# First attention of an attention-then-feed-forward kernel: roots on ScalarE, chunk additions on GpSimd, integer additions of the weights on VectorE

## The chip, the core and the metric

The kernel runs on one core of a Trainium2 chip. A core has five engines, each with its own queue of instructions, worked off strictly in order: TensorE (PE; its weight loads are shown as PEld), VectorE (DVE), ScalarE (ACT), GpSimd (POOL) and SyncE (SP, which here only issues DMAs). Engines wait for each other through semaphores. The metric is the device time of one execution in microseconds, the median of three runs.

## The reference

Attention over 8 batches and 12 heads, 448 tokens, 64 channels, with RMS norms of q and k; then a feed-forward block with a squared ReLU over the 3584 tokens.

```python
def rmsnorm(x, g):
    rms = np.sqrt(np.mean(x * x, axis=-1, keepdims=True) + 1e-06)
    return x / rms * g
q_n, k_n = (rmsnorm(q, g_q), rmsnorm(k, g_k))
scores = 1.0 / np.sqrt(64) * np.matmul(q_n, k_n.transpose(0, 1, 3, 2))
attn = np.exp(scores - np.max(scores, axis=-1, keepdims=True))
attn = attn / (np.sum(attn, axis=-1, keepdims=True) + 1e-09)
x = np.matmul(attn, v)           # (8, 12, 448, 64) -> (3584, 768)
...
h = x @ w_in                     # 768 -> 2048
g = np.maximum(h, 0.0) ** 2
out = g @ w_out                  # 2048 -> 768
```

The weights w_in and w_out come in double precision, everything else in single.

## The kernel before

**Stages.** The work goes in four spans of two batches each. A span has an attention over 12 pairs of heads, then the first product (with w_in, below "L1") and the second product (with w_out), both by a Strassen-like scheme of seven products of blocks in place of eight. Attention of the later spans is woven into the second product of the span before. The attention of the first span has nothing to be woven into: `attention_alone` runs it by itself, with `NAT` = 12 pairs, and L1 of span 0 follows. Beside these two stages the weights are prepared.

**One iteration of `attention_alone`** (pair i) is written out by hand as an order of instructions; each engine's queue has its share of it, in that order. There are four parts, with a `yield` behind each, and at each yield the caller puts in one or two quarter steps of the weight preparation:

1. scores of key chunks 0 and 1 (L771 on PE, into two PSUM tiles) and their exponentials (L775 on ACT, with k's root as the scale); the transposes of k of pair i+1 (L746 on PE, copied by L748 on ACT); the second half of the values of pair i-1 (L829); `add_up(i, 1)`, the sum of chunks 0 and 1 on DVE (L788); `norm(i + 2)`.
2. the transposes of q of pair i+1, moved to SBUF by ACT (L750); the load of the next v.
3. scores and exponentials of chunks 2 and 3; `total_of(i - 1)` on PE (L854): the sums of the exponentials over the keys, by matmuls with ones; the first half of the values; `finish(i - 1)` on DVE: a transpose of the totals (L867), their reciprocal (L868), a transpose back (L869) and the multiplication of the attention's result (L878).
4. in some iterations a second `add_up` on DVE; `combine_x(i - 1)`, sums for the products, on DVE (L888 to L893).

**The norm** (L702 to L711) squares q and k on ACT, sums on DVE (L703), scales and adds epsilon on DVE (L704), takes the power -0.5 on POOL (L706, 112 x 16 numbers) and multiplies q by it on POOL (L708). For pairs 0, 1 and 2 `normalise_in_turn` (L332 to L340) does the same for q and k one after the other, with q's multiplication on DVE.

**Totals.** `total_of` adds up by matmuls, two per tensor (each shows as two records): the DVE sum of chunks 0 and 1, and each chunk left. With odd i (but the last) the second `add_up` has put chunk 2 into the DVE sum too, so two tensors are left, 8 records; with even i and the last there are three, 12 records.

**Order of q.** q and k are loaded with four tokens in each of 112 partitions, so token 4p+j stands at column j*112+p behind the transposes; `finish` writes the result with a stride of four to bring the tokens back into order.

**The weights.** Each of 32 blocks of doubles is rounded to single precision by integer operations: ACT makes the high word's magnitude (L578) and scales the low word (L594), DVE clamps, shifts and joins (L591, L596, L601), and POOL adds both as integers, in two halves of 384 columns (`value`, L566). For every second block POOL makes four sums of blocks (`total`, L572), and SP writes seven block matrices to DRAM (w1s or w2s), from where the products load them as `sw`. A block takes four quarter steps: 13 blocks' worth (`EARLY` = 52 quarter steps) beside the first attention, the rest beside L1, at 88 quarter steps in 50 products.

**L1** (L1044 on PE). For each of eight f there are seven products of 6 matmul records, in the order pa, pb, pc, pd, pa, pd, pc by the names of the PSUM tiles. pb, pc and pd take two PSUM banks in turn, so pd takes the bank of pb, and may start when DVE has taken pb's result (L1051, into z). Other results are taken by L1054 and L1059 on DVE, and by ACT, which then does ReLU (L1016) and square (L1018).

Of the kernel before, what the change touches and what calls it, by code (L numbers as in the profile page):

```python
# [2 lines left out]

# [304 lines left out]
    return qk[:, first:second + 1:second - first]  # L308


def load_q(nc, qk, q, i):

    _, H, S, D = q.shape
    b, h0 = divmod(2 * i, H)
    nc.sync.dma_start(places_of(qk, i, 0)[:S // 4, 0].rearrange("p (h e) -> p h e", h=2),
                      q[b, h0:h0 + 2].rearrange("h (p j) d -> p h (j d)", j=4))
# [8 lines left out]
        nc.sync.dma_start(dst[:, :, h], k[b, h0 + h].rearrange("(p j) d -> p j d", j=4))  # L325


def normalise_in_turn(nc, raw, sq, rstd, mhalf, between=lambda: None):

    SP, _, n = rstd.shape  # L330
    for s in range(2):
        nc.scalar.activation(sq[:, s], raw[:, s], AF.Square)  # L332
        nc.vector.tensor_reduce(rstd[:, s], sq[:, s].rearrange("p (n d) -> p n d", n=n), AX, ALU.add)
        nc.vector.tensor_scalar(rstd[:, s], rstd[:, s], float(n) / sq.shape[2], 1e-6, ALU.mult, ALU.add)
        nc.gpsimd.tensor_tensor(rstd[:, s], rstd[:, s], mhalf[:SP, 0:n], ALU.pow)
        if s == 0:
            between()
            nc.vector.tensor_tensor(sq[:, 0].rearrange("p (j h d) -> p h j d", j=n // 2, h=2),
                                    raw[:, 0].rearrange("p (h j d) -> p h j d", j=n // 2, h=2),
                                    rstd[:, 0].rearrange("p (h j) -> p h j ()", h=2)  # L340
                                    .to_broadcast([SP, 2, n // 2, sq.shape[2] // n]), ALU.mult)


def first_pair(tc, q, k, g_q, g_k, held):
# [24 lines left out]
    with tc.tile_pool(name="ps_first", bufs=1, space=bass.MemoryType.PSUM) as ps_first:  # L369

        nc.vector.memset(qkT[:, 1], 0.0)
        idle = ps_first.tile([2 * D, S], F32, name="idle")
        for _ in range(3):
            nc.tensor.matmul(idle, qkT[:, 1, 0, 0:2 * D], qkT[:, 1, 1], start=True, stop=True)
        normalise_in_turn(nc, raw, sq, rstd, mhalf, between)
        for s, src in ((1, raw[:, 1]), (0, sq[:, 0])):
            pt = ps_first.tile([2 * D, S], F32, name=f"pt{s}")
            for j in range(NJ):
                nc.tensor.transpose(pt[:, j * SP:(j + 1) * SP], src[:, j * 2 * D:(j + 1) * 2 * D], ident[:SP, :SP])
            if s:  # L380
                nc.scalar.copy(qkT[:, 0, s], pt)
            else:
                nc.scalar.activation(qkT[:, 0, s], pt, AF.Copy, scale=gains[:, 0:1])


@with_exitstack
def attention_then_ffn_bounded(
# [128 lines left out]
    def blocks_of(n):  # L516
        at = n // 2 % BLOCKS * 8 * HW
        return stage[:, at:at + 8 * HW].rearrange("p (k m) -> p k m", k=8)

    def exponents_of(n):  # L520
        at = BLOCKS * 8 * HW + n % EXPS * NW
        return stage[:, at:at + NW]
# [23 lines left out]
    def prepare(t):  # L546
# [10 lines left out]
        def value(n, half):  # L557
            if not there(n):
                return

            to = ((A11, A12), (A21, A22)) if n < NFC else ((A11, A21), (A12, A22))
            dst = blocks_of(n)[:, to[n % 2][half]]
            part = slice(half * HW, (half + 1) * HW)
            if doubles:
                _, eu, low, _ = parts(n)
                nc.gpsimd.tensor_tensor(*[x.bitcast(I32) for x in (dst, low[:, part], eu[:, part])], ALU.add)  # L566
            else:
                nc.gpsimd.tensor_copy(dst, words_of(n).bitcast(F32)[:, part])

        def total(n, dst, x, y, op):  # L570
            if there(n) and n % 2:
                nc.gpsimd.tensor_tensor(*[blocks_of(n)[:, i] for i in (dst, x, y)], op)  # L572

        def unsigned(n):

# [7 lines left out]
        if there(n) and n % 2:  # L583
            c = n % NFC // 2
            dst = w1s[c] if n < NFC else w2s[:, c // 4, :, c % 4]
            nc.sync.dma_start(dst.rearrange("k p m -> p k m"), blocks_of(n)[:, 0:7])
            written[0] = n + 1
        if there(t) and doubles:
            e, eu, low, high = parts(t)
# [103 lines left out]
    def norm(i):  # L693
# [8 lines left out]
        nc.scalar.activation(sq, raw, AF.Square)  # L702
        nc.vector.tensor_reduce(rstd, sq.rearrange("p s (n d) -> p s n d", d=D), AX, ALU.add)  # L703
        nc.vector.tensor_scalar(rstd, rstd, 1.0 / D, 1e-6, ALU.mult, ALU.add)  # L704
        flat = rstd.rearrange("p s n -> p (s n)")
        nc.gpsimd.tensor_tensor(flat, flat, mhalf[:SP, 0:4 * NJ], ALU.pow)  # L706

        nc.gpsimd.tensor_tensor(sq[:, 0].rearrange("p (j h d) -> p h j d", j=NJ, h=2),  # L708
                                raw[:, 0].rearrange("p (h j d) -> p h j d", j=NJ, h=2),
                                rstd[:, 0].rearrange("p (h j) -> p h j ()", h=2).to_broadcast([SP, 2, NJ, D]),  # L710
# [31 lines left out]
    def transpose(i, s, n):  # L742

        pt = bank("pt", n)
        for j in range(NJ):
            nc.tensor.transpose(pt[:, j * SP:(j + 1) * SP], normed[i][s][:, j * P:(j + 1) * P], ident[:SP, :SP])  # L746
        if s:
            nc.scalar.copy(qkT[:, i % 2, s], pt)  # L748
        else:
            nc.scalar.activation(qkT[:, i % 2, s], pt, AF.Copy, scale=gains[:, 0:1])  # L750

    def scores(i, c):

# [26 lines left out]
    def add_up(i, c):  # L780

        acc = acc_of(i)
        if i >= NAT and c == NF:
# [2 lines left out]
                nc.vector.tensor_tensor(part, part, probs[i, c][rows], ALU.add)  # L786
            return
        nc.vector.tensor_tensor(acc, probs[i, 0] if c == 1 else acc, probs[i, c], ALU.add)  # L788

    def fold(i):  # L790

# [48 lines left out]
                    nc.tensor.matmul(into, vs[i][rows, h, c, :], probs[i, c][rows, h, :],  # L840
                                     start=(c == 0), stop=(c == NF), skip_group_check=True)

    def added(i):

        return 3 if i % 2 and i + 1 < NAT else 2

    def total_of(i):


        tots[i] = ps_o.tile([P, S], F32, tag="t", name="tot")  # L850
        parts = [acc_of(i)] + [probs[i, c] for c in range(added(i), NJ)]
        for n, pr in enumerate(parts):
            for h in range(2):
                nc.tensor.matmul(tots[i][h * D:(h + 1) * D, :], sums["ones"], pr[:, h, :],  # L854
                                 start=(n == 0), stop=(n + 1 == len(parts)))

    def finish(i):
# [4 lines left out]
        if i < NAT:  # L862
# [5 lines left out]
            nc.vector.reciprocal(few, turned.rearrange("p (g r) -> p g r", r=32)[:, :, 0])  # L868
            nc.vector.transpose(factors.rearrange("p (g r) -> p g r", r=32),  # L869
                                few.rearrange("p g -> p g ()").to_broadcast([P, S // 32, 32]))  # L870

            x = x.rearrange("d (p j) -> d j p", j=NJ)
            pav, factors = (t.rearrange("d (j p) -> d j p", j=NJ) for t in (pav, factors))
        else:
            rest = rests.pop(i)
            nc.vector.tensor_tensor(rest, pav, rest, ALU.add)
# [18 lines left out]
    def attention_alone():  # L895


        for i in range(NAT):
# [5 lines left out]
            if i == 0:  # L904
# [6 lines left out]
                norm(2)  # L911
                load_v(1)
                values(0, (0, 1))
                load(3)
                yield
                continue
# [10 lines left out]
            if more:  # L927
                transpose(i + 1, 0, 0)
            load_v(i + 1)
            yield  # L930
            scores(i, 2)
            scores(i, 3)
# [1 line left out]
            values(i, (0, 1))  # L934
            finish(i - 1)
            yield
            if added(i) == 3:
                add_up(i, 2)
            combine_x(i - 1)
            if NAT <= i + 3 < NAT + 2:  # L940
                load(i + 3)
# [210 lines left out]
    with tc.tile_pool(name="words", bufs=2) as spare["pool"]:  # L1152
# [5 lines left out]
        with tc.tile_pool(name="first", bufs=2, reuse_waits="tile") as work:  # L1158
# [1 line left out]
            free = [gT[:, f] for f in range(NFC) if f % HF < HF - 2]  # L1160
            places[:] = [g.rearrange("p (h q) -> p h q", h=2) for g in free[:2 * NJ]]
            sums[0], sums[1] = (g.rearrange("p (h q) -> p h q", h=2) for g in free[2 * NJ:2 * NJ + 2])
            sums["turned"], sums["factors"] = (g[:, 0:S] for g in free[2 * NJ + 2:2 * NJ + 4])
            sums["ones"] = work.tile([SP, D], F32, tag="ones", name="ones", bufs=1)
            nc.vector.memset(sums["ones"], 1.0)
            for u, _ in enumerate(attention_alone()):

                weights(min(EARLY, 4 + (EARLY - 4) * u // (4 * NAT - 7)))
# [39 lines left out]
def kernel(  # L1208
# [40 lines left out]
    )  # L1249
    with tc.manual_schedule():  # L1250

        nc.vector.memset(top, 0.0)
        nc.scalar.activation(top, top, AF.Exp)
        first_pair(tc, q, k, g_q, g_k, held)

    bits = nc.values_load(top.bitcast(mybir.dt.int32))
# [37 lines left out]
```

## Time and profile before

| what | value |
|---|---|
| median of three runs | 1365.82 us (1364.13 to 1366.27) |
| the profiled execution | 1362.09 us, its span on the core 1360.0 us |
| granted TensorE clock | 0.998 |
| instructions | 16939 |
| root on POOL, L706 | 9 x 3242 ns = 29.2 us |
| q's multiplication on POOL, L708 | 9 x 1413 ns = 12.7 us |
| integer additions on POOL, L566 | 34 x 1139 ns, 20 x 1226 ns, 10 x 1248 ns |
| block sums on POOL, L572 | 64 x 1167 ns = 73.5 us |
| chunk additions on DVE in the first attention, L788 | 17 x 1465 ns = 24.8 us |

A row names the line, the engine, the operation, what it writes and reads, and gives its count and the mean time of one. A duration holds everything from the start of the instruction on its engine to its end, so also the time in which a started instruction stands still for another engine. Starts are in microseconds from the beginning of the span. Neighbouring instructions of an engine overlap by some 0.1 us in the records. The page's busy shares are unions of such durations, over the whole span; windows give them for a stretch.

### The profile page before, as it was taken

The page shows a single profiled execution, that of the slowest core. Times are in us where ns is not written, and L with a number is a line of the kernel's source. Part 1 is how long each engine was busy: PE and PEld are TensorE (multiplying, and loading weights), DVE is VectorE, ACT ScalarE, POOL GpSimd, SP SyncE. Part 2 cuts the span into 40 slices and gives each one's busy share as a digit, 9 for nine tenths or more (in the row PEclk, how much of TensorE's full clock was granted, in tenths as well). Part 3 has the DMA queues.
Part 4 walks back from the last instruction along what each step waited for, and adds up shares of the span by engine and source line. Part 5 has one row for each costly group of instructions (what it writes and reads, how often), then busy time and mean ns, then how long its engine had stood idle before and what let it go on. Part 6 is the DMA issues. An engine that isn't in the chain of part 4 may idle for free.

```text
span 1360.0 us, 16939 instructions
## 1 busy us (share of the span) xinstructions
PE 1340.6 (99%) x5618; PEld 642.3 (47%) x5618; DVE 815.2 (60%) x1436; ACT 426.8 (31%) x657; POOL 636.8 (47%) x505
## 2 busy tenths in 40 slices
PE   8989999999999999999999999999999999999998
PEld 3333455444444455444444455444444455555554
DVE  6989776499987333567778523557788633332111
ACT  7876466433332011233332111233333211110000
POOL 6998887466573122655564222546566312220000
PEclk9999999999999999999999999999999999999999
DMA  9687999665675433355675433345665443234443
GB/s 250 192 235 196 300 379 330 180 132 110 130 149 127 102 89 88 96 119 118 137 150 114 113 100 87 101 104 117 144 128 111 103 103 87 87 91 107 104 114 70
DMA packets 434085, 190.12 MB, mean 140 GB/s; under 512 B 282949, under 2 KB 430789, under 8 KB 433989
## 3 DMA queue, kind: packets, MB, share of 16 engines
q1 hardware_dynamic: 427364, 180.33, 52.3%
q0 software_dynamic: 4736, 8.40, 2.4%
q8 instruction: 47, 0.77, 0.2%
q10 hardware_dynamic: 1888, 0.23, 0.1%
q14 instruction: 50, 0.40, 0.1%
HBM read 155.72 MB, written 33.16 MB: 139 GB/s over the span
## 4 chain that ended last, share of the span: by engine, by line
PE 89%; POOL 5%; DMA 2%; issue 2%; ACT 1%; SPq 0%; DVE 0%; ACTq 0%; POOLq 0%
PE ps L1110 37%; PE pd L1044 10%; PE pc L1044 10%; PE pa L1044 10%; PE sc L763 7%; PE pav L840 7%; PE pb L1044 5%; POOL gC L566 1%; POOL rstd L706 1%; POOL gC L572 1%; DMA sw<-w1s 1%; POOL qk L708 1%; PE sc L771 1%; ACT gT L775 1%; DMA qk<-in_k_dram 0%
## 5 line engine op out<-in xcount | busy, mean ns | idle before, releaser
L1110 PE MATMUL ps<-gT,sw 128*128 128x448 f32 x752 | 293.0, 543 | 0.0
L1020 POOL TENSOR_TENSOR gT<-gT 128x448 f32<-128x448 f32 x96 | 93.4, 975 | 282.9 <-ACT gT L1016 282.9
L1110 PE MATMUL ps<-gC,sw 128*128 128x448 f32 x576 | 225.2, 543 | 0.0
L1110 PEld LDWEIGHTS ps<-gT,sw 128*128 128x128 f32 x752 | 141.2, 190 | 146.3 <-issue 142.1
L728 POOL TENSOR_TENSOR half<-half,mhalf 128x28 f32<-128x28 f32 x36 | 175.1, 4863 | 73.4 <-DVE half L727 72.2
L1110 PEld LDWEIGHTS ps<-gC,sw 128*128 128x128 f32 x576 | 108.2, 190 | 112.8 <-issue 110.4
L1044 PE MATMUL pa<-xT,sw 128*128 128x448 f32 x384 | 155.0, 540 | 0.6 <-ACT p L1048 0.6
L1016 ACT ACTIVATE gT<-gT 128x448 f32<-128x448 f32 x96 | 55.4, 577 | 309.3 <-DVE gT L1059 309.3
L765 ACT ACTIVATE pr<-sc 128x896 f32<-128x896 f32 x87 | 77.5, 915 | 122.4 <-PE sc L763 122.2
L763 PE MATMUL sc<-qkT 64*64 64x448 f32 (+1 forms) x1152 | 109.8, 496 | 0.0
L1044 PEld LDWEIGHTS pa<-xT,sw 128*128 128x128 f32 x384 | 73.0, 190 | 72.5 <-issue 69.9
L808 POOL DMA_DIRECT2D xT<-factors x72 | 38.0, 532 | 92.8 <-DMA factors<-square 61.1
L1059 DVE TENSOR_TENSOR gT<-z,pd 128x448 f32<-128x448 f32 x32 | 19.9, 621 | 100.3 <-PE pd L1044 100.3
L1044 PE MATMUL pd<-xC,sw 128*128 128x448 f32 x192 | 77.5, 540 | 1.1 <-DVE gT L1059 1.1
L1044 PE MATMUL pc<-xC,sw 128*128 128x448 f32 x192 | 77.5, 540 | 0.4 <-DMA sw<-w1s 0.4
L730 POOL TENSOR_TENSOR qk<-qk,half 128x448 f32<-128x448 f32 x72 | 76.6, 1084 | 2.8
L1044 PE MATMUL pd<-xT,sw 128*128 128x448 f32 x192 | 77.8, 542 | 0.1
L1044 PE MATMUL pc<-xT,sw 128*128 128x448 f32 x192 | 77.5, 540 | 0.0
L1044 PE MATMUL pb<-xC,sw 128*128 128x448 f32 x192 | 77.4, 539 | 0.0
L572 POOL TENSOR_TENSOR gC<-gC 128x384 f32<-128x384 f32 x64 | 73.5, 1167 | 2.5
L840 PE MATMUL rest<-pr,vt 64*64 64x448 f32 x348 | 72.7, 537 | 0.0
L840 PE MATMUL pav<-pr,vt 64*64 64x448 f32 x348 | 72.7, 537 | 0.0
(138 smaller groups left out, 1900.0 us busy)
## 6 DMA issues: line engine op xcount, KB each, us to landing
sw<-w1s SPq DMA_DIRECT2D x224, 192.0 KB, 2.4
sw<-w2s SPq DMA_DIRECT2D x168, 256.0 KB, 3.3
w1s<-gC SPq DMA_DIRECT2D x8, 1344.0 KB, 7.7
w2s<-gC SPq DMA_DIRECT2D x8, 1344.0 KB, 8.2
out_dram<-osb SPq DMA_DIRECT2D x186, 56.0 KB, 1.8
qk<-in_q_dram SPq DMA_DIRECT2D x144, 56.0 KB, 3.6
qk<-in_k_dram SPq DMA_DIRECT2D x144, 56.0 KB, 2.8
xT<-factors POOLq DMA_DIRECT2D x72, 112.0 KB, 3.4
```

The source lines that it names most:

```text
L572: nc.gpsimd.tensor_tensor(*[blocks_of(n)[:, i] for i in (dst, x, y)], op)
L728: nc.gpsimd.tensor_tensor(half, half, mhalf, ALU.pow)
L730: nc.gpsimd.tensor_tensor(qkn[:, s], raw[:, s], half[:, s * NG:(s + 1) * NG].rearrange("p g -> p g ()").to_broadcast([P, NG, 32]), ALU.mult)
L763: nc.tensor.matmul(sc[part, h, 0:n], qkT[rows, 0, 1, keys], qkT[rows, 0, 0, of], start=True, stop=True)
L765: nc.scalar.activation(pr, sc[:, :, 0:n], AF.Exp)
L808: nc.gpsimd.dma_start(xT[h * D:(h + 1) * D, b % 2, hp], sums["out"][i % 2].rearrange("(h g) t -> h () (g t)", h=2)[h].to_broadcast([D, S]))
L840: nc.tensor.matmul(into, vs[i][rows, h, c, :], probs[i, c][rows, h, :], start=(c == 0), stop=(c == NF), skip_group_check=True)
L1016: nc.scalar.activation(g, src, AF.Relu)
L1020: nc.gpsimd.tensor_tensor(g, g, g, ALU.mult)
L1044: nc.tensor.matmul(ps, stream[n + at][:, c], rhs[:, c], start=first and c == 0, stop=c == HC - 1, skip_group_check=not first)
L1059: add(g, x, ps, ALU.add)
L1110: nc.tensor.matmul(ps, stream[n][:, c % 4], rhs_of[i][:, c], start=c == 0, stop=c == HF - 1)
```

## The change

- **Roots.** In the norms of pairs 3 to 11 the power on POOL goes. A new function `roots`, called for pair i+2 in part 2 of iteration i (behind q's transposes, ahead of the yield), computes it as exp(-0.5 ln) on ACT, and refines it by one Newton step of three small DVE instructions; q's multiplication on POOL follows there, some half part later in the order than before. The kernel's start loads a table that has both functions.
- **Chunks 2 and 3.** `add_rest(i)` adds them on POOL (112 x 896 numbers) in part 4, for all pairs but the last; the second `add_up` on DVE goes. `total_of` then has two tensors for all pairs but the last.
- **Token order.** ACT writes q's transposes with a stride of four, so that everything behind is in token order, and L878 has plain rows.
- **Squares of pairs 1 and 2** go from ACT to DVE (four instructions); pair 0 stays.
- **Weights.** For blocks 13 to 31, which fall beside L1, the two integer additions on POOL become one on DVE of 768 columns, right behind L601 of the next block. `place_of` shifts the blocks' places so that both halves can be written by one instruction; the DMA still writes seven blocks in a row.

```diff
 def normalise_in_turn(nc, raw, sq, rstd, mhalf, between=lambda: None, first=False):
...
+        if first:
+            nc.scalar.activation(sq[:, s], raw[:, s], AF.Square)
+        else:
+            nc.vector.tensor_tensor(sq[:, s], raw[:, s], raw[:, s], ALU.mult)
...
+    def place_of(n, k):
+        return 7 * int(n >= NFC) if k == A21 else k + int(n < NFC)
...
+            if n < EARLY // 4:
+                dst = blocks_of(n)[:, places[half]]
                 nc.gpsimd.tensor_tensor(*[x.bitcast(I32) for x in (dst, low[:, part], eu[:, part])], ALU.add)
+            elif half == 0:
+                dst = blocks_of(n)[:, places[0]:places[1] + 1:places[1] - places[0]]
+                low, eu = (x.rearrange("p (h m) -> p h m", h=2) for x in (low, eu))
+                nc.vector.tensor_tensor(*[x.bitcast(I32) for x in (dst, low, eu)], ALU.add)
...
+    def roots(i):
...
-        nc.gpsimd.tensor_tensor(flat, flat, mhalf[:SP, 0:4 * NJ], ALU.pow)
-
+        y, t = (small.tile([P, 2 * S // 32], F32, tag=tag, name=tag)[:SP, 0:4 * NJ] for tag in ("half", "other"))
+        nc.scalar.activation(y, flat, AF.Ln, scale=2.0 ** -63)
+        nc.scalar.activation(y, y, AF.Exp, scale=-0.5, bias=sums["rebias"])
+        nc.vector.scalar_tensor_tensor(t, y, -0.5, flat, ALU.mult, ALU.mult)
+        nc.vector.tensor_tensor(t, t, y, ALU.mult)
+        nc.vector.scalar_tensor_tensor(flat, t, 1.5, y, ALU.add, ALU.mult)
         nc.gpsimd.tensor_tensor(sq[:, 0].rearrange("p (j h d) -> p h j d", j=NJ, h=2),
...
-            nc.scalar.activation(qkT[:, i % 2, s], pt, AF.Copy, scale=gains[:, 0:1])
+            nc.scalar.activation(in_token_order(qkT[:, i % 2, s]), pt.rearrange("d (j p) -> d j p", j=NJ), AF.Copy,
+                                 scale=gains[:, 0:1])
...
+    def add_rest(i):
+        nc.gpsimd.tensor_tensor(sums["rest"][:SP], probs[i, 2], probs[i, 3], ALU.add)
...
-    def added(i):
-
-        return 3 if i % 2 and i + 1 < NAT else 2
...
-        parts = [acc_of(i)] + [probs[i, c] for c in range(added(i), NJ)]
+        parts = [acc_of(i)] + ([sums["rest"][:SP]] if i + 1 < NAT else [probs[i, c] for c in range(2, NJ)])
...
-            x = x.rearrange("d (p j) -> d j p", j=NJ)
-            pav, factors = (t.rearrange("d (j p) -> d j p", j=NJ) for t in (pav, factors))
...
             load_v(i + 1)
+            if i + 2 < NAT:
+                roots(i + 2)
             yield
...
-            if added(i) == 3:
-                add_up(i, 2)
+            if more:
+                add_rest(i)
             combine_x(i - 1)
...
-        nc.vector.memset(top, 0.0)
-        nc.scalar.activation(top, top, AF.Exp)
+        nc.scalar.preload_act_table_set("natural_log_exp_and_others")
```

## The prediction

> **What bounds the kernel now.** I read the page first (busy shares, slices), then the windows by stage, then TensorE's waits, and last the instructions one by one where VectorE and GpSimd meet.
>
> ```profile
> PE 1340.6 (99%) x5618; PEld 642.3 (47%) x5618; DVE 815.2 (60%) x1436; ACT 426.8 (31%) x657; POOL 636.8 (47%) x505
> PEclk9999999999999999999999999999999999999999
> ```
>
> TensorE (PE) is busy 99% of the span, at full clock. So a change can win only two things: the few gaps, and matmuls that go away. It can lose as much as it likes, by opening new gaps. The windows tell where gaps are (columns: stretch, length, busy time of PE, weight loads, VectorE = DVE, ScalarE = ACT, GpSimd = POOL, granted clock, DMA share, GB/s):
>
> ```profile
> 8.00:24.00 16.00, 13.21 (x69) 5.43 (x70) 9.80 (x18) 15.87 (x28) 9.21 (x5) 1.00 1.02 293
> 24.00:59.00 35.00, 35.00 (x184) 13.58 (x182) 33.63 (x43) 28.61 (x48) 31.61 (x18) 1.00 0.71 192
> 59.00:99.00 40.00, 35.54 (x178) 13.31 (x176) 32.55 (x41) 30.62 (x50) 39.29 (x27) 0.96 0.92 247
> 99.00:134.00 35.00, 33.69 (x176) 12.35 (x172) 32.60 (x44) 21.61 (x36) 30.40 (x18) 1.00 0.76 204
> 160.00:220.00 60.00, 60.00 (x161) 30.43 (x160) 42.93 (x55) 37.83 (x59) 47.64 (x48) 1.00 1.02 374
> ```
>
> The first attention runs to about 134 us. At its start ACT is the full engine (15.87 of 16.00), from 59 to 99 it is POOL (39.29 of 40.00), and DVE is above 80% all the way. L1, the first product, is gapless on PE from 160 on, with DVE at 42.93 of 60. The waits of PE, 8 to 264 us:
>
> ```profile
> PE pt L746 <- POOL qk L708: 4.9, 5, 2.3
> PE pt L746 <- ACT qkT L748: 1.9, 1, 1.9
> PE pd L1044 <- DVE gT L1059: 1.1, 1, 1.1
> PE pc L1044 <- DMA sw<-w1s: 0.4, 1, 0.4
> ```
>
> The largest, 4.9 us, is q's transposes waiting for POOL's normalised q (L708). It stands behind the root, L706, which takes 3242 ns nine times, 29.2 us. After the longest gap (2.3 us, at 91.6) the scores and totals also run slow: 2.38 and 2.75 us for the usual 1.76 and 1.73. So POOL's lateness costs 4.9 + 1.6 = 6.5 us.
>
> One resource stands on no line of the page. DVE, then POOL, 40 to 47 us:
>
> ```profile
> 40.09 1.91 DVE L788 TENSOR_TENSOR gT<-gT 112x896 f32<-112x896 f32 x1
> 43.16 0.81 DVE L704 TENSOR_SCALAR rstd<-rstd 112x16 f32<-112x16 f32 x1
> 43.88 0.55 DVE L596 TENSOR_SCALAR gC<-gC 128x768 uint32<-128x768 uint32 x1
> 44.46 0.96 DVE L601 SCALAR_TENSOR_TENSOR gC<-words,gC 128x768 uint32<-128x768 uint32 x1
> ```
> ```profile
> 39.70 1.35 POOL L566 TENSOR_TENSOR gC<-gT,gC 128x384 int32<-128x384 int32 x1
> 41.12 2.81 POOL L572 TENSOR_TENSOR gC<-gC 128x384 f32<-128x384 f32 x2
> 44.04 3.15 POOL L706 TENSOR_TENSOR rstd<-rstd,mhalf 112x16 f32<-112x16 f32 x1
> ```
>
> L788 alone takes 1.08; here 1.91, since it stands until L566 is over (41.05) and then needs its 1.08. L572 in turn stands until L788 is over (42.00). L704, 0.17 alone, takes 0.81 behind L572. The two engines take turns: a DVE instruction with two inputs in SBUF, or a plain L591, L596 or L704 from SBUF to SBUF, excludes a POOL addition. Under the root (44.04 to 47.19), L596 and L601 run at their free 0.55 and 0.96: **the root excludes nobody**. From 24 to 134 us the durations above the free ones sum to 17.9 us on DVE (L788 6.5, L596 2.7, L704 2.5, combines 2.2, L591 2.1, L601 1.9) and 18.1 us on POOL.
>
> The Trainium skill ("SBUF — State Buffer", section "Who interferes with whom") has the same exclusion for any GpSimd instruction that reads SBUF, so by it the root holds DVE off too. The trace above says it doesn't. By that rule nine roots less would free 29.2 us of the shared port against some 21 us of new additions, the first attention would run at PE's own pace, and the change would give about -9 us instead of the -4.3 below.
>
> **The change, part by part.**
>
> *Totals, on PE.* Six totals (even pairs 0 to 10) go from 12 records to 8; from start to the next start 23.40-25.71 (2.31) against 33.41-34.97 (1.56). 6 x 0.75 = 4.5 us of PE less. One iteration of the loop takes PE 9.26 without gaps (27.31 to 36.57); the nine from 27.31 to 120.66 took 93.35. PE's floor for the stretch is thus 9 x 9.26 = 83.3, 10 us less, if nobody else binds.
>
> *Roots.* POOL loses 29.2. ACT gets 18 small activations; no row shows Ln, the 1x1 Exp of L1253 took 202 ns, a 448-wide copy 556: between 0.2 and 0.55, nearest 0.2, so 0.4 per iteration. ACT has some 1 us of idle time per iteration there, but the logarithm stands in ACT's queue before the exponentials of chunks 2 and 3 and waits for DVE's mean (L704). In the iteration from 100.85, L704 ends at 107.7 and those exponentials start at 106.75; they would start near 108.2 and be done at 110.4, where the next scores want the PSUM at about 110.1 and 111.0. So it just fits, and I add nothing; the upper bound is 1 us in each of nine iterations. DVE gets 27 instructions like L726 (189 ns): 5.1 us.
>
> *Two chunks on POOL.* 384 columns take 1.00 (L572), 448 take 1.13 (the combines of later pairs): 2.03 ns per column, so 896 take 2.04; eleven make 22.4. POOL's sum is -29.2 + 22.4 = -6.8 us, and it is no longer the full engine between 59 and 99. But these 22.4 exclude DVE and the roots didn't. On DVE five L788 go: -5.4, and a third of their waiting, -2.2.
>
> *Token order.* The last multiplication, L878, takes 980 ns with its strided write; a contiguous one (L1051) 620: 11 x -0.36 = -4.0 us on DVE. The stride moves to ACT's q copy (L750, 654 ns); between 0 and 0.36 more each, and I take 0, hidden in ACT's idle time.
>
> *DVE's new waiting.* The low end is 0 (each addition lies under the 2.5 us of L867 to L878, which read PSUM or one tensor, as the root does today). The high end is that each of the 27 finds a POOL instruction under way and each addition is met by a DVE instruction, half of it still to come: 27 x 0.45 + 11 x 1.0 = 23. Nearest is today's mean, 17.9 us over 67 instructions that can be excluded, 0.27: 27 x 0.27 = 7.3, and for the additions, which hold on for nearly twice as long as L566 or L572, 11 x 0.45 = 5. DVE's sum: -5.4 - 2.2 - 4.0 + 5.1 + 7.3 + 5 = +5.8. DVE was busy 98.8 of the 110 us from 24 to 134; it would need about 104.6. **That is the new bound of the first attention: 104 to 105 instead of 110. I take -6** (bounds -10 by PE's floor, and +5 by the high end: 98.8 + 16.5 = 115).
>
> *Squares of pairs 1 and 2 on DVE.* Four activations of 0.65 leave ACT where it is full (8 to 24 us); four DVE instructions of 0.69 (L338's row) enter where it is 61% busy. The gap of 1.9 us behind L748 shrinks: -1.3 (bounds -1.9 and 0, since the logarithm of pair 3 comes in behind it).
>
> *Integer additions in L1.* For 19 of 32 weight blocks two POOL instructions (L566, 1.0 each) become one DVE instruction of 768 columns; L601's 0.95 is the row. POOL had room, so its 38 us are worth nothing at PE, but DVE pays 19 x 0.95 = 18 us in a stage where its order matters:
>
> ```profile
> 187.91 0.63 DVE L591 TENSOR_SCALAR gC<-gC 128x768 f32<-128x768 f32 x1 [2.05 <-ACT gC L578]
> 188.58 0.96 DVE L596 TENSOR_SCALAR bits<-gC 128x768 uint32<-128x768 uint32 x1
> 189.57 0.95 DVE L601 SCALAR_TENSOR_TENSOR gC<-gC,bits 128x768 uint32<-128x768 uint32 x1
> 190.45 0.61 DVE L1051 TENSOR_TENSOR z<-p,pb 128x448 f32<-128x448 f32 x1
> ```
>
> Behind L601 now comes the addition, and then L1051, which frees the bank that PE wants for pd at 191.67. L1051 ends at 191.06 today; one addition makes it 192.0, and a second one before L591 (which waits for ACT behind L1059) makes it 193.0. PE waits 0.3 to 1.4 us there. The weight steps shift against the products from f to f; where L1051 falls before L601 nothing is lost. I take 0.5 for each of six f: **+3** (bounds 0 and +10). DMAs are the same in number and size; the write of w1s, which follows POOL's sums, is not later.
>
> *The table preload* replaces a load of 1283 ns by another: 0.
>
> **Sum:** -6 - 1.3 + 3 = -4.3. The profiled execution took 1362.1 (span 1360.0), so 1357.8 for one like it; the three timed runs have their median 3.7 above it, so 1361.5. About 0.2% (2.7 us) is what a measurement can tell from no change.
>
> **Rivals.**
> 1. *DVE in L1 becomes the bound* (slower). For: DVE's own work per f (three weight steps of 2.5 + 0.95, five results of 0.62) is 13.5 of 15.8 us, and it waits some 2 us for L578 after L1059 in most f. Against: PE's waits there are small today. Price: 1.9 us in each of 6 f = 11, so -7.3 + 11 = +4, 1370; it decides once the stall exceeds 7.3 / 6 = 1.2 us per f.
> 2. *PE's floor is reached*: the additions lie under L867 to L878 as the roots do. -10 - 1.3 + 1 = -10, 1355.5. Against: DVE was above 80% already.
> 3. *No difference*: the shared port binds, the attention gains 2 and L1 loses 3: 1365.
> 4. *The change doesn't do what it says*: Ln and Exp alternate their tables. 18 loads of 1.28 = 23 us on ACT, less 1 us of idle time in nine iterations: +14, with the rest 1375. The Trainium skill ("ScalarE: Activation LUTs", section "Table sets: the hidden batching unit") lists one set with both, which no row here shows.
>
> **How the numbers follow.** Forecast 0.45, rival 1 0.28, rival 2 0.15, rival 3 0.08, rival 4 0.04. Of the forecast's cases (1357 to 1365) four in five lie over 0.2% below, the rest within. Faster 0.36 + 0.15 = 0.51; same 0.09 + 0.08 + 0.04 of rival 1 = 0.21; slower 0.28. Range: 1353.5 to 1372. The forecast's own: 1357 to 1365.
>
> **What would show it.** Right: iterations of 9.4 to 9.8 between the first scores, no wait of PE for L708, totals of 8 records, DVE over 93% until 130, small waits of pd for L1051 in L1. Wrong: PE waiting for pb or pd by over 1 us in each f (rival 1); attention over before 125 (rival 2); ACT table loads in the loop (rival 4); PE waiting for scores' PSUM behind the logarithm.

## The result and the profile after

The changed kernel takes **1375.71 us** (median of 4 runs, 1375.17 to 1377.2) against 1365.07 for the kernel before (4 runs on the same chip): ratio 1.0079, 95% interval 1.0062 to 1.0097. It is slower by 0.8%, and outside the predicted range of 1353.5 to 1372. The profiled execution took 1375.17, its span is 1373.4. It is compared with the profiled execution of before (1362.09), so the profiles show a difference of 13.1 us where the medians show 10.6.

Where the time came from is read from two starts, those of L1's first matmul (into pa) and of the first scores of span 1, first before, then after:

```profile
134.43 2.52 PE L1044 MATMUL pa<-xT,sw 128*128 128x448 f32 x6
264.10 1.74 PE L763 MATMUL sc<-qkT 64*64 64x448 f32 x16
```
```profile
146.44 2.52 PE L1076 MATMUL pa<-xT,sw 128*128 128x448 f32 x6
276.91 1.73 PE L795 MATMUL sc<-qkT 64*64 64x448 f32 x16
```

L1 begins at 134.4 us before and at 146.4 after: **+12.0 in the first attention**. L1 itself went from 129.7 to 130.5. All else adds 0.6 to the span. The page's busy line of the kernel after:

```profile
PE 1343.6 (98%) x5594; PEld 640.0 (47%) x5594; DVE 844.2 (61%) x1481; ACT 433.7 (32%) x670; POOL 589.5 (43%) x469
```

POOL has 47 us less work over the span (636.8 before) and DVE 29 us more (815.2). PE's 24 records fewer are the six totals that went from 12 to 8. The windows of after, in the columns of the prediction:

```profile
8.00:24.00 16.00, 13.66 (x67) 5.52 (x64) 11.43 (x23) 13.50 (x21) 10.17 (x6) 0.89 1.02 290
24.00:59.00 35.00, 31.80 (x156) 11.54 (x154) 33.28 (x45) 28.03 (x50) 25.93 (x18) 0.95 0.67 187
59.00:99.00 40.00, 34.07 (x162) 12.17 (x158) 38.00 (x50) 30.86 (x53) 33.49 (x25) 0.94 0.82 239
99.00:134.00 35.00, 32.26 (x158) 11.73 (x158) 34.03 (x39) 28.15 (x49) 29.23 (x21) 0.97 0.68 181
160.00:220.00 60.00, 58.50 (x155) 29.09 (x154) 49.12 (x63) 37.84 (x58) 22.41 (x22) 1.00 0.99 362
```

From 59 to 99 POOL, full before (39.29 of 40), has room now, and DVE is at 38.00 of 40. PE is gapless nowhere in the first attention; its granted clock is 0.89 in the first of these stretches and 0.94 to 0.97 in the next three. The prediction had this bound (its sign, DVE over 93% until 130, came: 95, 95 and 97% in the three stretches from 24 us on), but not its price. Now the whole first attention from 24 us to the start of L1 in one line, first of before, then of after:

```profile
24.00:134.40 110.40, 104.63 (x530) 39.25 (x526) 99.18 (x127) 80.84 (x133) 101.71 (x61) 0.98 0.80 216
```
```profile
24.00:146.40 122.40, 107.77 (x512) 38.43 (x508) 116.84 (x152) 90.05 (x154) 95.11 (x63) 0.94 0.72 197
```

DVE's busy time went from 99.18 to 116.84, 17.7 us more. PE's idle time went from 5.8 (110.40 - 104.63) to 14.6. PE's busy time rose by 3.1 although the totals have 24 records fewer, since its matmuls run slower between the gaps (the scores below are one case). Three of PE's waits in the kernel after, 8 to 280 us, and the wait of ACT that stands behind the first of them, 24 to 147 us (columns: total, times, longest):

```profile
PE sc L803 <- ACT gT L807: 9.0, 5, 2.5
PE pt L777 <- ACT qkT L779: 2.9, 5, 1.0
PE tot L886 <- DVE gT L899: 2.8, 1, 2.8
```
```profile
ACT half L734 <- DVE rstd L725: 18.9, 9, 3.7
```

The wait for L708 (4.9 us before) is gone. Instead the scores wait 9.0 us for PSUM that the exponentials (L807) have not emptied; the exponentials stand in ACT's queue behind the logarithm (L734), and that waits 18.9 us for DVE's mean (L725).

One such place, 76 to 88 us. DVE, then POOL:

```profile
78.45 1.90 DVE L820 TENSOR_TENSOR gT<-gT 112x896 f32<-112x896 f32 x1
80.28 1.21 DVE L724 TENSOR_REDUCE rstd<-qk 112x16 f32<-112x1024 f32 x1
81.52 0.80 DVE L725 TENSOR_SCALAR rstd<-rstd 112x16 f32<-112x16 f32 x1
```
```profile
76.38 3.03 POOL L584 TENSOR_TENSOR gC<-words,gC 128x384 int32<-128x384 int32 x2
79.48 2.80 POOL L592 TENSOR_TENSOR gC<-gC 128x384 f32<-128x384 f32 x2
```

ACT in the same stretch:

```profile
82.35 0.21 ACT L734 ACTIVATE half<-rstd 112x16 f32<-112x16 f32 x1 [3.69 <-DVE rstd L725]
82.60 0.31 ACT L735 ACTIVATE half<-half,rebias 112x16 f32<-112x16 f32 x1
82.81 2.19 ACT L807 ACTIVATE gT<-sc,rstd 112x448 f32<-112x448 f32 x4
```

And PE:

```profile
84.01 3.21 PE L803 MATMUL sc<-qkT 64*112 64x448 f32 x8 [2.53 <-ACT gT L807]
```

L820 needs 1.08 alone and takes 1.90 behind an integer addition of POOL. L725 needs 0.17 and takes 0.80, behind two block sums that POOL ran from 79.48 to 82.28. With L725 the logarithm is late (ACT idle for 3.69), behind it the exponentials, and PE stands for 2.53 us. The eight scores that follow take 3.21 for the usual 1.76. Here the loss is made on DVE; ACT's queue and PE only carry it. POOL's instructions in this place are ones that the kernel before has too; what the eleven additions do is told by the experiments.

Summed as in the prediction, from 24 us to the start of L1, the durations above the free ones on DVE (its waiting) were 18.2 us before and are 35.8 after (on L820 10.4, L617 6.6, L622 6.4, L612 4.6, L725 3.5, the 27 root instructions 2.4, the combines 1.8). The groups that bear on it, 24 to 147 us of after:

```profile
L820 DVE TENSOR_TENSOR gT<-gT 112x896 f32<-112x896 f32 x11 | 24.2, 2202 | 0.8 <-ACT gT L807 0.8
L824 POOL TENSOR_TENSOR gT<-gT 112x896 f32<-112x896 f32 x11 | 26.2, 2382 | 0.2 <-ACT gT L807 0.2
L739 POOL TENSOR_TENSOR qk<-qk,rstd 112x512 f32<-112x512 f32 x9 | 11.6, 1292 | 20.3 <-ACT half L735 9.2 <-ACT gT L807 6.4 <-ACT gT L615 3.7
L781 ACT ACTIVATE qkT<-pt,gains 128x448 f32<-128x448 f32 x10 | 11.2, 1118 | 1.9 <-PE pt L777 1.8
```

L820 stands at twice its free time, a mean of 2202 ns. In front of L739 POOL is idle for 20.3 us, 9.2 of them put down to the root's exponential (L735).

### The profile page after: what moved, and what is told of

Same layout as the page of the kernel before. It is cut to its first block, busy times and chain, and to the rows that moved or that the text cites. A ratio compares the mean times of both kernels' runs of the same rounds, so it can differ in the third digit from the quotient of the medians.

```text
span 1373.4 us, 16850 instructions
## 1 busy us (share of the span) xinstructions
PE 1343.6 (98%) x5594; PEld 640.0 (47%) x5594; DVE 844.2 (61%) x1481; ACT 433.7 (32%) x670; POOL 589.5 (43%) x469
## 4 chain that ended last, share of the span: by engine, by line
PE 88%; DVE 8%; ACT 2%; issue 1%; POOL 0%; DMA 0%; DVEq 0%; ACTq 0%; POOLq 0%
PE ps L1142 37%; PE pd L1076 10%; PE pa L1076 10%; PE pc L1076 10%; PE sc L795 7%; PE pav L876 7%; PE pb L1076 5%; DVE gT L820 1%; DVE gC L622 1%; DVE rstd L724 1%; DVE gC L612 1%; ACT gT L807 1%; DVE gC L617 1%; PE ps L1127 0%; DVE rstd L725 0%
## 5 line engine op out<-in xcount | busy, mean ns | idle before, releaser
L1142 PEld LDWEIGHTS ps<-gC,sw 128*128 128x128 f32 x576 | 108.0, 190 | 113.1 <-issue 110.3
L592 POOL TENSOR_TENSOR gC<-gC 128x384 f32<-128x384 f32 x64 | 70.2, 1113 | 62.8 <-DVE gC L588 61.0
```

Source lines behind the costliest of these rows:

```text
L592: nc.gpsimd.tensor_tensor(*[blocks_of(n)[:, place_of(n, i)] for i in (dst, x, y)], op)
L1142: nc.tensor.matmul(ps, stream[n][:, c % 4], rhs_of[i][:, c], start=c == 0, stop=c == HF - 1)
```

## The experiments

**Theories.** TURNS: the eleven additions on POOL hold off DVE, which has no time to spare, and that is the loss. QUEUE: the logarithm, which waits for DVE ahead of the exponentials in ACT's queue, is the loss. Two more came up on the way. LATE RESULT: the totals wait for POOL's sum. GPSIMD TIME: any work of that length on POOL costs as much. All kernels were timed in three rounds beside the kernel before, which had medians of 1364.5 (e1 to e4), 1362.8 (e5 to e8) and 1363.05 (e9 to e12) in the three groups of runs. So kernels of different groups are compared by their ratios.

| kernel | time, us | ratio, 95% interval | L1 starts at | DVE's waiting |
|---|---|---|---|---|
| before | 1365.07 | | 134.4 | 18.2 |
| after | 1375.71 | 1.0079 (1.0062, 1.0097) | 146.4 | 35.8 |
| e1_pow | 1384.92 | 1.0143 (1.0126, 1.016) | 155.9 | 28.6 |
| e2_late | 1381.54 | 1.0122 (1.0105, 1.0139) | 152.8 | 32.3 |
| e3_dveadd | 1362.26 | 0.9984 (0.9974, 0.9994) | 132.9 | 19.4 |
| e4_poolint | 1374.37 | 1.0068 (1.0051, 1.0085) | 144.9 | 35.8 |
| e5_idle_add | 1378.91 | 1.0118 (1.0101, 1.0135) | 149.5 | 36.2 |
| e6_idle_pow | 1364.67 | 1.0009 (1.0, 1.0019) | 135.3 | 23.5 |
| e7_noadd_late | 1365.57 | 1.0017 (1.0006, 1.0027) | 135.5 | 22.4 |
| e8_noadd_noorder | 1362.75 | 1.0 (0.9991, 1.001) | 135.6 | 16.5 |
| e9_add_only | 1383.61 | 1.0156 (1.0139, 1.0173) | 154.8 | 24.8 |
| e10_roots_only | 1360.75 | 0.9985 (0.9975, 0.9994) | 131.9 | 16.8 |
| e11_half | 1363.77 | 1.0006 (0.9996, 1.0016) | 134.3 | 27.8 |
| e12_noadd_nostep | 1359.75 | 0.9975 (0.9964, 0.9986) | 130.8 | 14.5 |

The last two columns are from one profiled execution each, which lies up to 3 us from its kernel's median (1362.09 before, 1377.52 in e4, 1365.38 in e8); DVE's waiting is the sum explained above.

**e1_pow: the change with the power back on POOL, at its old place.**

```diff
-        nc.scalar.activation(y, flat, AF.Ln, scale=2.0 ** -63)
-        nc.scalar.activation(y, y, AF.Exp, scale=-0.5, bias=sums["rebias"])
...
+        nc.gpsimd.tensor_tensor(flat, flat, mhalf[:SP, 0:4 * NJ], ALU.pow)
...
                 norm(i + 2)
+                roots(i + 2)
```

> The changed kernel (1375.7 us against 1365.1 before) with the roots undone: the power is back on GpSimd, at its old place in the norm; everything else stays changed. Theory TURNS: the chunk additions on GpSimd exclude VectorE's additions and the small operations; VectorE is full (its waiting for turns grew from 17.9 to 38 us), and that is the loss. By it the roots' 27 small VectorE instructions go (some 7 us with their waiting), but GpSimd gets 29 us more on top of 89 of 110 us and is full itself: 1372 to 1380. Theory QUEUE: the logarithm stands in ScalarE's queue ahead of the exponentials of chunks 2 and 3 and waits 18.9 us for VectorE's mean (L725); so the exponentials are late, TensorE waits 9.0 us for them and runs at a lower clock behind each wait. By it the loss is gone: 1363 to 1367.

1384.92, slower than the changed kernel. QUEUE falls as the whole cause, since no logarithm is in ACT's queue any more. TURNS had the direction and missed the size: with powers and additions together POOL is the full engine (103.9 of the 110 us from 24 to 134), and the totals wait for its sums:

```profile
PE tot L881 <- POOL gT L819: 17.9, 9, 4.5
```

**e2_late: the change with the roots behind `finish`,** so that the exponentials of chunks 2 and 3 stand ahead of the logarithm.

```diff
             load_v(i + 1)
-            if i + 2 < NAT:
-                roots(i + 2)
...
             finish(i - 1)
+            if i + 2 < NAT:
+                roots(i + 2)
```

> The changed kernel with the call of roots moved behind the scores and exponentials of chunks 2 and 3 and behind finish, so the logarithm can hold up no exponential of its iteration. Theory QUEUE: TensorE's 9.0 us of waits for the exponentials and the slow clock behind them go: 1363 to 1367. Theory TURNS: VectorE has the same work and the same turns: 1372 to 1376.

1381.54: against both. With the queue's obstacle gone the kernel is slower still, since q's multiplication, behind the roots, now comes late, and with it POOL's additions:

```profile
PE pt L777 <- POOL qk L739: 8.5, 4, 3.7
PE tot L886 <- POOL gT L824: 8.0, 3, 3.8
```

**e3_dveadd: the change without the additions on POOL** (the second `add_up` and three-tensor totals as before).

```diff
-        parts = [acc_of(i)] + ([sums["rest"][:SP]] if i + 1 < NAT else [probs[i, c] for c in range(2, NJ)])
+        parts = [acc_of(i)] + [probs[i, c] for c in range(added(i), NJ)]
...
-            if more:
-                add_rest(i)
+            if added(i) == 3:
+                add_up(i, 2)
```

> The changed kernel without the chunk additions on GpSimd: as before, VectorE adds chunk 2 for every second pair, and the totals have 12 or 8 records. TensorE has 4.5 us more of matmuls, VectorE five additions of 1.08 more. Theory TURNS: the 26 us in which the additions exclude VectorE go and with them most of the added 20 us of waiting: 1363 to 1367. Theory QUEUE: the logarithm stands where it stood, its wait is only as much shorter as VectorE is less late: 1371 to 1376.

1362.26, 0.16% faster than before: all of the loss is gone. L1 starts at 132.9, DVE's waiting is 19.4, the logarithm stays where the change put it. QUEUE falls as the main cause: the logarithm still waits for DVE, 12.8 us, but PE's wait for the exponentials is down from 9.0 to 2.9.

```profile
ACT half L734 <- DVE rstd L725: 12.8, 9, 2.6
```
```profile
PE sc L803 <- ACT gT L807: 2.9, 4, 1.0
```

The traces also show what POOL ran while a DVE instruction stood. In the changed kernel 14.0 us of DVE's waiting lie beside the additions, 11.5 beside the block sums (L592) and 9.2 beside the integer additions (L584). Without the additions it is 8.1 beside the sums and 10.0 beside L584. TURNS holds so far, but two other readings of this run were left: the totals' wait for POOL's result, and POOL's time. From 24 us to L1 in this kernel:

```profile
24.00:132.90 108.90, 103.79 (x530) 38.73 (x526) 103.16 (x157) 89.28 (x153) 71.08 (x52) 1.00 0.79 222
```

**e4_poolint: the change with L1's integer additions back on POOL.**

```diff
-            if n < EARLY // 4:
+            if n < 2 * NFC:
```

> The changed kernel with the integer additions of blocks 13 to 31 back on GpSimd, as two instructions of 384 columns. It tells what the first product pays for them on VectorE. Both theories put the whole loss into the first attention, where the stage before L1 is 12.1 us longer and L1 itself only 0.7: 1374 to 1376.5. Were the prediction's rival 1 right (VectorE full in L1), it would be 1365 to 1370.

1374.37; its interval overlaps that of the changed kernel, so this part of the change makes no difference that these runs show. In its profile, of its slowest run, L1 took 134.1 us (130.5 in after); three waits for loads of w1s there come to 4.2 us, the largest of them

```profile
PE pd L1076 <- DMA sw<-w1s: 2.7, 1, 2.7
```

This profile also bounds what the slow clock is worth. DVE's waiting is 35.8 here as in the changed kernel, but the granted clock from 24 us to L1 is 0.99 in place of 0.94, and L1 starts 1.5 us earlier, no more:

```profile
24.00:144.90 120.90, 103.37 (x509) 36.98 (x507) 115.85 (x151) 89.15 (x153) 93.68 (x63) 0.99 0.73 200
```

**e5_idle_add: e3 with the eleven additions put back on POOL, whose result nobody reads.**

```diff
                 values(0, (0, 1))
+                add_rest(0)
...
+            if more:
+                add_rest(i)
             if added(i) == 3:
                 add_up(i, 2)
```

> The kernel without the chunk additions on GpSimd (e3_dveadd, 1362.3 us), and beside it the same eleven additions of 112 x 896 on GpSimd after all, at their old place in its queue, with a result that nobody reads. So no engine waits for these additions any more; they only take GpSimd's time and exclude VectorE. Theory TURNS (they exclude VectorE, which is full): VectorE's waiting for turns goes from 19 to about 35 us again, and the time to 1372 to 1380. Theory LATE RESULT (the totals wait for the additions, so the exponentials' places and TensorE do): 1362 to 1364. Theory GPSIMD TIME (what stands behind the additions in GpSimd's queue is late: q's multiplication, the weights): 1370 to 1380.

1378.91: the loss is back without a single instruction waiting for the sums, and is larger than in the change, since here DVE's second `add_up` stays too. LATE RESULT isn't needed for the loss.

```profile
24.00:149.50 125.50, 110.58 (x536) 40.35 (x532) 120.96 (x156) 89.72 (x154) 98.17 (x63) 0.96 0.67 192
```
```profile
L824 POOL TENSOR_TENSOR gT<-gT 112x896 f32<-112x896 f32 x11 | 28.0, 2546 | 0.3 <-ACT gT L807 0.2
```

DVE's instructions are those of e3, and its waiting rose from 19.4 to 36.2, by 16.8; L1 starts 16.6 later. That is 1.53 us of DVE's time for one addition, by the sum from 24 us on. The first addition falls ahead of it, in this kernel and in the changed one, and holds L820 for 1.9 more. In the changed kernel:

```profile
23.07 2.09 POOL L824 TENSOR_TENSOR gT<-gT 112x896 f32<-112x896 f32 x1
```
```profile
23.12 2.99 DVE L820 TENSOR_TENSOR gT<-gT 112x896 f32<-112x896 f32 x1
```

**e6_idle_pow: e5 with a power of 112 x 10 numbers in the place of each addition.**

```diff
-        nc.gpsimd.tensor_tensor(sums["rest"][:SP], probs[i, 2], probs[i, 3], ALU.add)
+        nc.gpsimd.tensor_tensor(sums["rest"][:SP, 0, 0:10], probs[i, 3][:, 0, 0:10], mhalf[:SP, 0:10], ALU.pow)
```

> As e5_idle_add, but in the place of each idle addition GpSimd takes the power of 112 x 10 numbers of the same exponentials (3.24 us for 16 of them and 1.65 for 8, so about 2.0, the addition's length), with a result that nobody reads. In the profile of before a power excluded nobody. Theory TURNS: VectorE's waiting stays near 19 us: 1362 to 1365. Theory GPSIMD TIME: the same as e5_idle_add within 2 us.

```profile
L824 POOL TENSOR_TENSOR gT<-gT,mhalf 112x10 f32<-112x10 f32 x11 | 26.5, 2410 | 0.0
```

The same eleven places, about as long on POOL (2410 ns against 2546), and 1364.67 in place of 1378.91. GPSIMD TIME falls. What costs is what POOL does in that time: the addition, with 896 numbers in each partition, holds DVE off; the power, with 10, does so little (DVE's waiting is 23.5, 4 us above e3, and only 1.7 of it lies beside the powers). Whether the amount of numbers or the kind of operation decides, these runs don't separate.

**e7_noadd_late: e3 with the roots behind `finish`** (the edit of e2).

> e3_dveadd (1362.3 us) with the call of roots moved behind the exponentials of chunks 2 and 3 and behind finish. In e3_dveadd TensorE still waits 2.9 us for exponentials and 2.9 for k's copies on ScalarE, which stand behind the logarithm's wait. If the logarithm's place costs what those waits are: 1356 to 1360. In e2_late the same move made the changed kernel 6 us slower, since q's multiplication came late behind it (TensorE waited 8.5 us for it) in a GpSimd queue with the additions; if that holds without them too: 1363 to 1368.

1365.57, slower than e3 by the ratios (1.0017 against 0.9984). Even with DVE relieved, the roots' place in the change is the better one; later, q is late again (L777 waits 6.1 us for L739). Since q moves with the roots here and in e2, neither run tells what the logarithm's place costs by itself.

**e8_noadd_noorder: e3 with q's old order.**

```diff
-            nc.scalar.activation(in_token_order(qkT[:, i % 2, s]), pt.rearrange("d (j p) -> d j p", j=NJ), AF.Copy,
-                                 scale=gains[:, 0:1])
+            nc.scalar.activation(qkT[:, i % 2, s], pt, AF.Copy, scale=gains[:, 0:1])
...
+            x = x.rearrange("d (p j) -> d j p", j=NJ)
+            pav, factors = (t.rearrange("d (j p) -> d j p", j=NJ) for t in (pav, factors))
```

> e3_dveadd (1362.3 us) with q in the order of before: ScalarE's copy of q has plain rows again (1118 ns with the stride, 641 before: 11 x 0.48 = 5 us of ScalarE), and VectorE's last multiplication writes with a stride (980 ns for 625: 4 us of VectorE). If ScalarE's time is what TensorE waits for (2.9 + 2.9 us of its waits are for ScalarE): 1358 to 1361. If VectorE, 95% busy, is: 1364 to 1367.

1362.75, between the two expectations. Its ratio is 1.0 against 0.9984 for e3, and the intervals just overlap: the runs don't tell the two apart. The token order takes 4 us from DVE and gives 5 to ACT; a gain or loss from it isn't shown.

**e9_add_only: the kernel before with the additions on POOL and nothing else.**

```diff
-            if added(i) == 3:
-                add_up(i, 2)
+            if more:
+                add_rest(i)
```

> The kernel before (1363 to 1365 us) with the chunk additions on GpSimd as its only change: eleven additions there, no second addition on VectorE, totals of 8 records for all pairs but the last. Roots, order of q, squares and weights as before. Theory TURNS: GpSimd has 31.6, 39.3 and 30.4 us busy in stretches of 35, 40 and 35 and gets 22 us more; VectorE is excluded for 22 us more, while TensorE saves 4.5: 1375 to 1386, much like e1_pow (1384.9). Theory of the prediction (the additions lie under VectorE's operations from PSUM, GpSimd alone is short of time): some 1368.

1383.61, inside the range of TURNS. Here POOL, which still has the powers, is the full engine:

```profile
24.00:154.80 130.80, 110.45 (x509) 39.69 (x505) 103.69 (x123) 80.69 (x134) 120.89 (x72) 0.91 0.68 184
```

**e10_roots_only: the kernel before with the roots on ACT and nothing else** (the function `roots`, its call and the table; the weight blocks' places are shifted as in the change).

> The kernel before with the roots by logarithm and exponential as its only change: order of q, squares, totals and integer additions as before (the blocks' places stay shifted, which is no instruction). GpSimd loses 29 us, VectorE gets 27 small instructions, ScalarE 18. In the profile of before TensorE lost 4.9 us to GpSimd's late q, and 1.6 to the clock behind it. If the roots win these: 1358 to 1361. If VectorE's small instructions (7 us with their waiting) and the logarithm's wait on ScalarE take it back: 1363 to 1366.

1360.75, 0.15% faster than before. The roots are the part that wins; the change without the additions (e3, 0.9984) is no faster.

**e11_half: the change with the additions for odd pairs only,** five of the eleven.

```diff
-            if more:
+            if more and i % 2:
                 add_rest(i)
```

> The changed kernel with the additions on GpSimd for odd pairs alone (5 of 11); the even pairs have totals of 12 records. By TURNS the loss goes with the number of additions: e3_dveadd is at 1362.3 and the changed kernel at 1375.7, 1.2 us for each addition, so 1366 to 1370. If the loss comes only where VectorE has no time left at all, it is nearer to one end: under 1364.

1363.77. Five additions bring DVE's waiting from 19.4 to 27.8 (1.7 each), the other six bring it to 35.8 (1.3 each): the waiting grows about evenly. But the time doesn't, and so the forecast by the number of additions (1366 to 1370) missed: the ratio goes from 0.9984 to 1.0006 and then to 1.0079, L1's start from 132.9 to 134.3 and then to 146.4. The two kinds of pairs differ in what leaves DVE. An odd pair's addition replaces a second `add_up`, 1.08 us of DVE's work; an even pair's takes only four records from PE, which had time. So DVE gets 8.4 - 5.4 = +3.0 from the first five and +8.0 from the other six, and 1.9 more from L820 at 23.12, whose addition is pair 0's. Its busy time in this kernel,

```profile
24.00:134.30 110.30, 104.27 (x530) 38.26 (x526) 105.56 (x150) 89.47 (x153) 80.29 (x57) 1.00 0.77 217
```

is 2.4 above e3 (103.16) and 11.3 below the change (116.84); L1's start moves by 1.4 and 12.1 in the same two steps. So L1's start goes with DVE's whole sum, not with the number of additions.

**e12_noadd_nostep: e3 without the Newton step.**

```diff
-        nc.scalar.activation(y, y, AF.Exp, scale=-0.5, bias=sums["rebias"])
-        nc.vector.scalar_tensor_tensor(t, y, -0.5, flat, ALU.mult, ALU.mult)
-        nc.vector.tensor_tensor(t, t, y, ALU.mult)
-        nc.vector.scalar_tensor_tensor(flat, t, 1.5, y, ALU.add, ALU.mult)
+        nc.scalar.activation(flat, y, AF.Exp, scale=-0.5, bias=sums["rebias"])
```

> e3_dveadd (1362.3 us) without the Newton step: the exponential's result is the root, as ScalarE's tables give it, so the refinement of the norm is left out, and 27 small instructions on VectorE go (5 us, some 2 of waiting). If VectorE still binds the first attention: 1356 to 1360. If TensorE's waits for ScalarE (5.8 us) come from the place of the logarithm: 1361 to 1363.

1359.75, inside the range expected if DVE still binds. But against e3 the ratios, 0.9975 and 0.9984, have intervals that overlap; in the profiles L1 starts 2.1 us earlier. So a gain from the 27 small DVE instructions less is likely, not shown. From 24 us to L1 DVE falls to 94.9 of 106.8 us and PE is busy for 104.4 of them; so PE's own work is what is left there.

```profile
24.00:130.80 106.80, 104.41 (x537) 39.15 (x533) 94.94 (x130) 89.53 (x153) 70.75 (x52) 1.00 0.83 226
```

**Read together,** DVE's busy time from 24 us to L1 goes with L1's start in the change and its close relatives. e3: 103.2 busy in 108.9 (PE, with 103.8, is as full there). e11: 105.6 in 110.3. e5: 121.0 in 125.5. After: 116.8 in 122.4. The rest is 4.5 to 5.7 each time, and from e3 to the change DVE's sum grows by 13.7 and L1's start by 13.5. Before, it was 99.2 in 110.4: DVE was not yet the bound there; POOL had 101.7, was full from 59 to 99, and PE waited for it. It isn't a law: in e2, where q is late, the rest is 15.7 with no engine full.

```profile
24.00:152.80 128.80, 110.18 (x516) 40.63 (x512) 113.07 (x152) 89.77 (x154) 97.93 (x63) 0.91 0.67 188
```

## Why the prediction was wrong

Its step that failed is **"DVE's new waiting"**, and in it the term of 5 us for the eleven additions ("for the additions, which hold on for nearly twice as long as L566 or L572, 11 x 0.45 = 5"). The runs put 16.4 us there (35.8 with the additions, 19.4 without, e3), or 16.8 (e5). That is one and a half times even the upper bound that I gave it, 11 x 1.0. I had taken a mean over instructions of a kernel in which DVE still had gaps: a DVE instruction that meets no POOL instruction today counts as zero in that mean. Beside a DVE queue almost without gaps an addition of 2.04 us cost DVE 1.5 us on average, three quarters of its length.

The second fault is in the line that follows it, "104 to 105 instead of 110". I set the length of the stretch equal to DVE's sum. In the kernels where DVE's sum and L1's start go together, 4.5 to 5.7 us of the stretch are not DVE's (e3, e11, e5, after). With my own sum of 105 that makes 110.5, no gain at all. The two together: DVE's sum +17.7 for my +5.8 is 11.9, and 5.6 for the rest of the stretch; that is 17.5 of the 18 between my -6 and the +12.0 measured, which lies outside my bounds of -10 to +5 as well. (The range's end, 1372, was in turn lower than my own upper bounds add up to: +5 here and +10 in L1 make about 1380.) The 11.9 are 16.3 too little for the additions and 4.4 too much for the rest: from before to e3 DVE's sum rose by 4.0, where the terms of the token order and the roots (-4.0, +5.1, +7.3) gave 8.4; from e3 to the change it rose by 13.7, where the terms of the additions (-5.4, -2.2, +5) gave -2.6.

The other steps, in the prediction's order:

- *What bounds it, and the turns:* right. The page's shares don't show it; the one-by-one view of DVE and POOL did, and it named the resource on which the loss was made.
- *The root excludes nobody:* right. In the kernel before none of DVE's 18.2 us of waiting lies beside L706, and in e6 1.7 of 23.5 lie beside the eleven powers. The rule of the Trainium skill ("SBUF — State Buffer", section "Who interferes with whom"), that a DVE instruction with two SBUF inputs contends with a GpSimd instruction that reads SBUF, holds here for the additions (1.53 us each, e5). For the power, which reads SBUF too and is as long, eleven put L1's start off by 2.4 us in all (e6), so by these runs the length of a GpSimd instruction doesn't say how long it holds the port. The prediction saw this, and then put 5 us on the exchange of 29.2 us that exclude nobody for 22.4 (26.2 measured) that do.
- *Totals:* 8 records for even pairs, as said, 24 records in all. PE's 4.5 us were of no use, since DVE was the bound.
- *Roots:* the 27 small instructions own 4.7 us (5.1 said) and wait 2.4 (7.3 said). That the logarithm "just fits" ahead of the exponentials fails in the changed kernel, where it waits 18.9 us, and the prediction's last sign of being wrong, PE waiting for scores' PSUM behind the logarithm, came with 9.0 us. But it carries DVE's lateness: without the additions it waits 12.8 us in the same place and nothing is lost (e3), and roots and q moved away together gain nothing (e2, e7).
- *Chunks on POOL:* the free time of 2.04 us was about right (the shortest took 2.08); POOL is no longer full. Both without worth.
- *Token order:* L907 at 625 ns, the -4.0 on DVE was right. The stride costs ACT 0.46 a copy (L781, 1118 ns against 654), above the bound of 0.36; the times don't show it (e8).
- *Squares:* PE's idle time from 8 to 24 us goes from 2.79 to 2.34, a gain of 0.45 for 1.3, and the lower clock there (0.89 for 1.00) takes it back: the first totals start at 24.45 after and at 23.40 before. In e3, at a clock of 1.00, they start at 23.26.
- *Integer additions in L1:* +0.8 for +3, inside its bounds. Rival 1, the slower one, had the right engine in the wrong stage: in L1 PE's waits for DVE come to 2.3 us in all.
- *The table:* rival 4 falls, no loads in the loop; that its price, 1375, is what was measured is an accident. Rival 2's condition, additions that lie under L867 to L878, failed: of the additions' 26.2 us 2.3 lie beside these instructions (now L899 to L907), 9.1 beside L820 and the rest beside others that DVE had at the time.

The cause is settled as far as the runs go: additions on POOL cost DVE's time, and DVE was the next bound behind POOL. Not tried was to place the additions so that they lie under DVE instructions that are not excluded.

## What to carry to other kernels

Before work is moved to an engine that shares a path with another, ask which of the two is full behind the change, and price each moved instruction on the full one by its length (three quarters of it in this case), not by the mean of today's collisions. A stretch is not as short as the sum of its bound engine: take into account what that engine leaves idle in a kernel where it binds. Try the parts of a mixed change alone; here the roots by themselves (e10, 1360.75, ratio 0.9985 with the interval's end at 0.9994) were faster than both kernels, and the additions with their totals started L1 13.5 us later than in the same kernel without them (e3).

## What the runs showed of the hardware that was not expected

- A power on POOL of 2.41 us leaves DVE nearly undisturbed; an addition of about the same time takes 1.53 us from it: DVE's waiting is 4.1 us above e3 with eleven powers and 16.8 above with eleven additions (e6, e5).
- ACT's copy of 448 columns from PSUM to SBUF takes 1118 ns with its result at a stride of four numbers, and 654 without.
- That scores run slow behind a wait was known from before; its weight was not. From 24 us to L1 the granted clock was 0.94 against 0.98, and the 160 score records from 24 to 134 us took 40.4 us against 35.9: 4.5 more, half of the 9.0 us that PE waited for the exponentials. Of L1's start it was little, 1.5 us between the change and e4.
